# An FFN beside attention on one core: the weight operands of TensorE moved to different starting bytes

## The chip, the cores and the metric

The kernel runs on one core of a Trainium2 chip. The core has five engines that run side by side: TensorE (PE; its weight loads are listed apart as PEld), VectorE (DVE), ScalarE (ACT), GpSimd (POOL) and SyncE (SP), which here issues the transfers. Operands lie in an on-chip memory of 128 partitions; a tile takes the same bytes in each partition, so "address" below means a byte within a partition. The metric is device time in microseconds of one execution; smaller is better.

## The reference, cut to what matters

Two branches read the same x (2048 rows, 576 columns, fp32) and are mixed row by row with a sigmoid gate:

```
g = sigmoid((x * gate_w).sum(-1))
a = attention(x)            # 32 heads of 18, four segments of 512 rows, softmax inside a
                            # segment and a running memory across segments, then @ wo
b = (silu(x @ w_gate) * (x @ w_up)) @ w_down     # 576 -> 4608 -> 576
out = g * a + (1 - g) * b
```

The change touches the operands of branch b only: `w_gate`, `w_up` and `w_down`.

## The kernel before

All matrix products of the projections and of the FFN are done in split form. An fp32 operand becomes a high part (ScalarE copies it to the format `F32R`) and a low part (VectorE subtracts the high part from the original); three products, high by high, high by low and low by high, are added in PSUM.

The kernel has four stages. Up to about 229 us the projections q, k, v are computed (`qk`, `v_step`, both through `products`, line 138). From there the FFN runs in two halves of 1024 rows, up to about 935 and 1640 us, and the attention of all segments is dealt out between its matmuls. At the end the attention's output is multiplied by `wo` (again line 138) and mixed with the FFN's sums.

**The FFN's gate and up (line 1034).** `F` = 4608 is cut into 36 blocks of 128 columns (`f`). For one block the two halves of rows and the two matrices gate and up form a two by two problem, which is computed with seven products in place of eight: seven combinations of weights (`wops`, `j` = 0 to 6) against seven combinations of x (`XO[j]`). One product is six matmuls at line 1034 (two row tiles `z`, each with high·high, high·low, low·high) and a seventh at line 1037 for the last 64 rows of D (`rem`, tiles `rh0` and `rh1`). The weights are the **stationary** operand (128x128), x is **streamed** past them (512 columns).

The tile of one combination of weights is `wo_`, made by `op_tile` (line 216), 2048 bytes per partition: high and low part of two row tiles. The pool `wop` holds seven such places, taken in turn, and ahead of them `rh0` and `rh1`. In the first half the tiles are made by `w_make`: GpSimd forms sums (`total`, line 247), ScalarE writes the high part (line 251), VectorE the low part (line 254), and SP stores the tile to `wc` in DRAM (line 257). In the second half `w_fetch` (line 703) loads them from there. Four places also hold raw x for a while before the second half (`x_second`, line 1004).

**The FFN's down product (line 893).** `down_group` multiplies the activations `hh`, `hl` (stationary) by the split down weights `dw` (streamed, 320 or 256 columns): nine matmuls for three blocks `f`, three per block, into one PSUM bank, and VectorE adds the result to `ya` (line 898). `dw` holds high and low part side by side, 2 x 576 numbers or 4608 bytes; the pool `fp` has three places of it. `d_split` makes one in the first half, and SP stores it to `dc`; `d_fetch` loads it in the second.

**The order of the work** is written out by hand. `tick` and `beat` are called after each of the seven products; they run what `defer` put into a list for that beat (loads, splits, stores), then up to three groups of the down product and at times a step of the attention generator `att_gen`. So behind a product at 1034 and 1037 there follows another product, a group at 893, or bf16 matmuls of attention (lines 727, 748, 769, 798, 800).

**Addresses.** Pools are stacked from two ends. From the low end: the ring (1024 bytes), `consts`, `xo` (x and its combinations), `rw`, `fp` (`hh`, `hl`, `draw`, `dw`), `yp` (`ya`). From the high end: `base` (32 bytes), `rp` (raw weights), `wop`, and below it the attention's pools. Within a pool tiles lie in the order of their first request. Two small tiles, `gap` in `consts` and `base`, are there only to shift what follows. With these sizes `xo`, `hh`, `hl`, `dw`, `ya`, `rh` and `wo_` all begin on byte 192 modulo 256.

Of the kernel before, what the change touches and what calls it, by code (L numbers as in the profile page):

```python
# [12 lines left out]
F32 = mybir.dt.float32  # L13
F32R = mybir.dt.float32r
# [6 lines left out]
P = 128  # L21
S = 2048
D = 576
H = 32
DH = 18
L = 512
# [37 lines left out]
def gated_mix(ctx, tc, xT, xrest, wf, wfr, wfh, wd, wv, wo, beta, cmask, ident, bmask, out):  # L64
    nc = tc.nc
# [133 lines left out]
    def raw_tile():  # L199
        return rp.tile([P, L], F32, name="raw")  # L200
# [12 lines left out]
    wraw_of, wops, rhs = {}, {}, []  # L213

    def op_tile():
        return wop.tile([P, 2, 2, P], F32R, name="wo_")

    def r_block(h, o):
        i, c = divmod(h, 2)
# [19 lines left out]
    def w_make(f):  # L239
        g, u = wraw_of.pop(f)  # L240
        ops = wops[0, f] = [None] * 7
        a11, a12, a21, a22 = g[:, 0:2], g[:, 2:4], u[:, 0:2], u[:, 2:4]
        src = [a11, None, None, a12, None, None, a22]

        def total(j, p, q, sub=True):
            src[j] = rp.tile([P, 2, P], F32, name="ws", bufs=3)
            (nc.gpsimd.tensor_sub if sub else nc.gpsimd.tensor_add)(src[j], p(), q())  # L247

        def high(j):
            ops[j] = op_tile()  # L250
            nc.scalar.activation(ops[j][:, 0], src[j], AF.Copy)

        def low(j):
            nc.vector.tensor_sub(ops[j][:, 1], src[j], f32(ops[j][:, 0]))

        def keep(j):
            nc.sync.dma_start(wc[f, j], f32(ops[j]).rearrange("p a k n -> p (a k n)"))

        todo = [(LEAD - 1, lambda: total(1, lambda: a21, lambda: a22, False)),
                (LEAD, lambda: total(2, lambda: src[1], lambda: a11)),  # L260
                (LEAD + 2, lambda: total(4, lambda: a11, lambda: a21)),
                (LEAD + 4, lambda: total(5, lambda: a12, lambda: src[2]))]
        for j in range(7):
            todo += [(LEAD + j, lambda j=j: high(j)), (LEAD + j + 2, lambda j=j: low(j)),
                     (LEAD + j + 3, lambda j=j: keep(j))]
        return sorted(todo, key=lambda t: t[0])
# [3 lines left out]
    with ExitStack() as st:  # L270
# [192 lines left out]
        for kt in range(NT):  # L463
            if kt % 2 == 0:
                both = staging(), staging()
            a = both[0][:, L * (kt % 2):L * (kt % 2) + 3 * P].rearrange("p (m n) -> p m n", n=P)
# [118 lines left out]
        for s in range(NSEG):  # L585
            upd = upd_gen(s - 1) if s else None
            casts = []
            for n, (m, u) in enumerate(chains):
                mid = []
                if s == 0:  # L590
                    for z in loads.get(n, []):
                        z()
                    if 0 < n < 6:
                        mid.append(lambda n=n: q_split(*chains[n + 3]))
                    if n in halves:
                        mid.append(lambda n=n: v_split(*halves[n]))
                if s == 1 and n < 3:
                    cast = masks(*((0, 3), (3, NT), (0, 0))[n])
                    casts.append(cast)
                if s == 1 and 3 <= n < 6:  # L600
                    mid.append(casts[n - 3])
                if (s, n) == (1, 7):
                    mid.append(betas)
                if (s, n) == (0, 3):
                    b_load(0)
                if (s, n) > (0, 3) and blocks:
                    mid.append(lambda z=blocks.pop(0): b_step(*z))
                if 1 <= s < 3:
                    if n == 2:
                        rest_load(2 - s)  # L610
                    for j in RSTEP.get(n, ()):
                        mid.append(lambda j=j: rest_split(2 - s, j) if j >= 0 else rest_sum(-j))
                if s == 3:
                    if 2 <= n < 6:
                        first_load(n - 2)
                    for j, z in FSUM.get(n, []):
                        mid.append(lambda j=j, z=z: first_sum(j, z))
                    for j, z in FSPLIT.get(n, []):
                        mid.append(lambda j=j, z=z: first_split(j, z))
                if s < 3:  # L620
                    for kt in ((0, 1), (2, 3), (4,))[n - 6] if s == 0 and n > 5 else (n - 4,) if s and n > 3 else ():
                        raws["x", kt] = x_load(s + 1, kt)
                qk(s, m, u, mid)
                flush(2)
                if upd is not None and n > 0:
                    next(upd, None)
            if s == 3:
                qst_.close()
                rp = pool(ctx, "rp", 4, side="right")
                wop = pool(ctx, "wop", 7, side="right")  # L630
                kq = pool(ast, "kq", 1, side="right")
                for i in range(NST):
                    if i < 2:
                        qst.append(kq.tile([P, 2, L], BF, name=f"qst{i}"))
                    if i < NST - 1:
                        kst.append(kq.tile([P, 2, L], BF, name=f"kst{i}"))
                for i in range(2):
                    mbs.append(kq.tile([P, 8], F32, name=f"mb{i}"))
                for z in range(2):
                    for j, b, kt in ((0, 2, z), (3, 2, 2 + z), (5, 3, 2 + z)):  # L640
                        XO[j][z] = xs_of[b][0][kt]
                wraw_of[0] = [w_load(0, u) for u in range(2)]
                for z in range(2):
                    rhs.append(wop.tile([P, 7, P], F32R, name=f"rh{z}", bufs=1))
                start = w_make(0)
            for n in range(8):
                hf, i = divmod(n, 4)
                flush()
                v_step(s, hf, i)
                if s:  # L650
                    mem_step(s, n // 2, n % 2)
                if s < 3:
                    if n == 0:
                        xs_of[s + 1] = x_tiles(s + 1)
                    if 1 <= n < 6:
                        x_split(xs_of[s + 1], n - 1, raws["x", n - 1])
                else:
                    if n == 4:
                        wraw_of[1] = [w_load(1, u) for u in range(2)]
                    if n < 2:  # L660
                        first_sum(6, n)
                    elif n < 6:
                        if n < 4:
                            nc.gpsimd.memset(f32(rhs[n - 2][96:]), 0.0)
                        if 3 <= n < 5:
                            r_fetch(n - 3)
                        if n - 2 < len(kst):
                            nc.gpsimd.memset(kst[n - 2], -1.0)
                    if n > 2:
                        for z in stack_loads(0)[2 * n - 6:2 * n - 4]:  # L670
                            nc.sync.dma_start(*z)
                    for _ in range((0, 0, 2, 3, 3, 3, 3, 3)[n]):
                        if start[0][0] < 8:
                            start.pop(0)[1]()
# [7 lines left out]
    with ExitStack() as st:  # L682
# [9 lines left out]
        fp = pool(st, "fp", CH)  # L692
# [174 lines left out]
                nc.sync.dma_start(*z)  # L867

        def d_tile():
            return fp.tile([P, 2, D], F32R, name="dw")  # L870

        def d_split(f, r):
            d = d_tile()
# [124 lines left out]
        def x_second(new, rest):  # L998
            r = {}
            todo = []  # L1000

            def load(z, q):
                b, kt = ((0, z), (1, z), (0, 2 + z), (1, 2 + z))[q]
                r[z, q] = wop.tile([P, L], F32, name="wo_") if z else raw_tile()[:, :L]
                nc.sync.dma_start(r[z, q], xT[HALF[1][b], :, kt])

            def total(z, j):
                c, d, e, g = (r.get((z, q)) for q in range(4))
                o, p, q = {1: (c, d, c), 4: (d, g, d), 2: (g, g, c), 6: (e, e, g)}[j]
                nc.gpsimd.tensor_sub(o, p, q)  # L1010

            def parts(z, j):
                new[j][z] = x_slot(SLOT[j], z)
                split(new[j][z][:, 0], new[j][z][:, 1], r[z, (0, 0, 3, 2, 1, 3, 2)[j]])

            def fetch(j):
                rest[j] = xr_tile(j)
                nc.sync.dma_start(f32(rest[j]), xrd[j])

            todo += [(o, lambda z=z, q=q: load(z, q)) for o, z, q in LOADS]  # L1020
            todo += [(o, lambda z=z, j=j: parts(z, j)) for o, z, j in PARTS]
            todo += [(o, lambda z=z, j=j: total(z, j)) for o, z, j in SUMS]
            todo += [(6 + j, lambda j=j: fetch(j)) for j in range(7)]
            return sorted(todo, key=lambda t: t[0])
# [17 lines left out]
        for pos, (half, f) in enumerate(seq):  # L1042
            if f == 0:
                yas[half] = yp.tile([P, 8, D], F32, name="ya")
            q = f % CH
# [186 lines left out]
```

## Time and profile before

| | |
|---|---|
| median of 3 runs | 1804.82 us (1804.8 to 1804.99) |
| span of the profiled execution, first to last instruction | 1803.0 us |
| around the span (median less span) | 1.8 us |
| granted TensorE clock, mean | 0.997 |
| PE busy, 0 to 229 us / 229 to 935 / 935 to 1640 / 1640 to 1803 | 221.38 / 696.21 / 703.67 / 157.84 us |
| ACT busy, the same stretches | 147.15 / 400.62 / 362.00 / 50.21 us |
| POOL busy, the same stretches | 106.84 / 316.07 / 380.90 / 28.52 us |
| DMA share, the same stretches | 0.57 / 0.69 / 0.56 / 0.52 |

The profiled execution is one execution on the chip with every instruction's start and duration; its own time is known here only as its span, to which the 1.8 us around it are added for a comparison with the runs. Matmuls overlap, and their recorded ends are modelled, so a busy PE says little by itself: what counts is the distance from one matmul's start to the next one's. The chain of work that ended last, listed in order of time, gives just this, since each piece in it lasts until the next piece starts. In its rows stand the start, the length, the engine with the tile written, the line, and how many instructions were merged.

### The profile page before, as it was taken

The numbers are of one execution on the slowest core, as the hardware profiler recorded it, in microseconds if no ns is written. First come the engines' busy times: TensorE is split into PE (matmuls) and PEld (weight loads), VectorE is DVE, ScalarE is ACT, GpSimd is POOL, SyncE is SP. The second block draws the span as 40 slices with busy tenths as digits, with TensorE's granted clock in tenths as the row PEclk, the third lists the DMA queues.
The fourth block names the chain that finished last, engine by engine and source line by source line (L and its number), as shares of the span: only waits on it lengthen the run. The fifth ranks groups of instructions, "written<-read, shape, count | busy, mean of one in ns | idle before, by whom it ended". The sixth has DMA issues, their size and how long they took to land.

```text
span 1803.0 us, 36363 instructions
## 1 busy us (share of the span) xinstructions
PE 1779.1 (99%) x12444; PEld 1529.7 (85%) x12444; DVE 1269.7 (70%) x3257; ACT 960.0 (53%) x1799; POOL 832.3 (46%) x1065
## 2 busy tenths in 40 slices
PE   9999999999999999999989999999999999999999
PEld 7898978888888888888877888888887887888899
DVE  6566566778877777777777767777777777764455
ACT  7666564465556555655546465355355355354511
POOL 4434632345554455345535555555555555553121
PEclk9999999999999999999999999999999999999999
DMA  8643496777657756776478456466455455456644
GB/s 289 215 174 141 148 324 205 229 260 264 186 198 248 256 181 193 246 247 193 160 262 247 137 176 195 135 172 195 124 179 181 144 168 180 137 160 187 199 137 139
DMA packets 244073, 352.01 MB, mean 195 GB/s; under 512 B 83440, under 2 KB 125680, under 8 KB 243888
## 3 DMA queue, kind: packets, MB, share of 16 engines
q1 hardware_dynamic: 243888, 349.68, 60.3%
q8 instruction: 99, 1.62, 0.4%
q14 instruction: 86, 0.70, 0.1%
HBM read 210.72 MB, written 138.87 MB: 194 GB/s over the span
## 4 chain that ended last, share of the span: by engine, by line
PE 92%; DVE 2%; DMA 2%; ACT 2%; issue 1%; SPq 0%; POOL 0%; ACTq 0%; DVEq 0%
PE bank L1034 36%; PE bank L893 25%; PE bank L138 11%; PE bank L1037 6%; PE bank L769 4%; PE bank L727 4%; PE bank L798 2%; PE bank L800 1%; PE bank L446 1%; PE bank L400 1%; DMA wo__23682<-wc 0%; DVE xo L116 0%; DMA stk<-q 0%; PE bank L332 0%; DMA raw<-in_xT_dram 0%
## 5 line engine op out<-in xcount | busy, mean ns | idle before, releaser
L893 PE MATMUL bank<-dw,hh 128*128 128x320 f32 (+1 forms) x2304 | 486.5, 304 | 6.0 <-DVE ya L898 4.4
L863 POOL TENSOR_TENSOR p<-pe,p 128x512 f16<-128x512 f32 x320 | 382.7, 1196 | 155.5 <-DVE p L861 107.1
L893 PEld LDWEIGHTS bank<-dw,hh 128*128 128x128 f32 x2304 | 377.9, 189 | 24.8 <-DVE ya L898 6.3
L773 ACT ACTIVATE pe<-bank 128x512 f32<-128x512 f32 x320 | 190.3, 595 | 313.9 <-PE bank L769 285.5
L893 PE MATMUL bank<-dw,hl 128*128 128x320 f32 (+1 forms) x1152 | 340.2, 295 | 0.3 <-DVE hl L116 0.3
L781 POOL TENSOR_SCALAR_AFFINE_SELECT pe<-pe 128x256 f32<-128x256 f32 (+1 forms) x320 | 137.5, 430 | 293.7 <-ACT pe L773 289.8
L734 DVE CUSTOM_DVE_ANT_0 scr<-bank,cm 128x512 bf16<-128x512 f32 (+3 forms) x512 | 247.8, 484 | 20.0 <-PE bank L727 12.0
L898 DVE TENSOR_TENSOR ya<-bank,ya 128x320 f32<-128x320 f32 x352 | 157.9, 453 | 113.2 <-PE bank L893 110.8
L893 PEld LDWEIGHTS bank<-dw,hl 128*128 128x128 f32 x1152 | 217.6, 189 | 0.9 <-DVE hl L116 0.9
L1037 PE MATMUL bank<-xr,rh 128*128 128x512 f32 x504 | 196.8, 391 | 0.0
L861 DVE CAST p<-pe 128x512 f16<-128x512 f32 x320 | 152.3, 476 | 0.0
L769 PE MATMUL bank<-qst,kst 111*128 111x512 bf16 (+3 forms) x512 | 150.9, 303 | 0.0
L727 PE MATMUL bank<-kst,qst 108*128 108x512 bf16 (+3 forms) x512 | 126.0, 300 | 0.6 <-DVE mb L734 0.5
L247 POOL TENSOR_TENSOR ws<-raw 128x256 f32<-128x256 f32 x72 | 66.2, 920 | 108.0 <-DMA raw<-in_wf_dram 51.7
L977 DVE TENSOR_TENSOR hl<-row,hh 128x512 fp32r<-128x512 f32 x120 | 99.7, 831 | 18.9 <-ACT hh L976 18.4
L1037 PEld LDWEIGHTS bank<-xr,rh 128*128 128x128 f32 x504 | 94.7, 188 | 20.3
L1101 ACT ACTIVATE row<-bank 128x512 f32<-128x512 f32 x72 | 43.1, 599 | 122.3 <-PE bank L1037 122.3
L1106 DVE TENSOR_TENSOR row<-bank,row 128x512 f32<-128x512 f32 x72 | 49.8, 691 | 81.8 <-ACT bank L1105 81.8
L1116 DVE TENSOR_TENSOR row<-bank,row 128x512 f32<-128x512 f32 x72 | 49.7, 690 | 64.2 <-PE bank L1037 51.5
L1105 ACT ACTIVATE bank<-bank 128x512 f32<-128x512 f32 x72 | 41.9, 582 | 97.9 <-PE bank L1037 94.8
L138 PE MATMUL bank<-xo,qhi 128*128 128x512 f32 x264 | 83.1, 396 | 0.0
L1098 DVE TENSOR_TENSOR bank<-bank,row 128x512 f32<-128x512 f32 x72 | 50.2, 697 | 41.6 <-PE bank L1037 33.4
(1702 smaller groups left out, 4040.3 us busy)
## 6 DMA issues: line engine op xcount, KB each, us to landing
rh<-rc SPq DMA_DIRECT2D x72, 336.0 KB
dc<-dw SPq DMA_DIRECT2D x36, 576.0 KB
dw<-dc SPq DMA_DIRECT2D x36, 576.0 KB
raw<-in_wf_dram SPq DMA_DIRECT2D x72, 256.0 KB
stk<-q SPq DMA_DIRECT2D x32, 384.0 KB
draw<-in_wd_dram SPq DMA_DIRECT2D x36, 288.0 KB
rc<-rt SPq DMA_DIRECT2D x42, 224.0 KB
vd<-vps SPq DMA_DIRECT2D x8, 912.0 KB
```

The source lines that it names most:

```text
L138: nc.tensor.matmul(t, st[n], mv[n], start=(n == 0), stop=(n == 13))
L727: nc.tensor.matmul(t[:, c:c + w], qs[:KR, pr, P * i:P * i + P], ks[:KR, pr, 0:w], start=True, stop=True)
L734: nc.vector.tensor_tensor_reduce(scr[:, :w], t[:, c:c + w], cm[:, L - w:L], 1.0, -3.0e38, OP.add, OP.max, m[:, k:k + 1])
L769: nc.tensor.matmul(t[:, c:c + w], ks[:KR + 3, pr, P * j:P * j + P], qs[:KR + 3, pr, P * j:L], start=True, stop=True)
L773: nc.scalar.activation(pe, t, AF.Exp, scale=SCALE)
L781: nc.gpsimd.affine_select(d, d, pattern=pat, compare_op=OP.is_ge, fill=0.0, base=0, channel_multiplier=-1)
L861: nc.vector.tensor_copy(p1, pe)
L863: nc.gpsimd.tensor_sub(p2, pe, p1)
L893: nc.tensor.matmul(t, p, q[:, cs], start=(n == 0), stop=(n == 3 * CH - 1))
L898: nc.vector.tensor_add(ya[:, i, cs], t, ya[:, i, cs])
L1034: nc.tensor.matmul(t, w[:, p, z], x[z][:, q], start=first and n == 0, stop=False, skip_group_check=True)
L1037: nc.tensor.matmul(t, rem[:, RPOS[j]], XR[j], start=False, stop=True, skip_group_check=True)
```

## The change

It changes the size of two kinds of tiles, adds one small tile, and shrinks a reserved area. The tiles keep their shapes for all instructions: eight more numbers (32 bytes) are reserved behind each and cut off again in the same line. `wo_` grows from 2048 to 2080 bytes, so its seven places lie 2080 bytes apart; `dw` grows from 4608 to 4640 bytes. Eight numbers of `gap` stand between `rh1` and the first `wo_`. Together `wop` is 256 bytes longer (7 x 32 + 32), so that the pools below it move by a whole turn of 256. `dynamic_dma_scratch_size`, the ring at the low end of the memory, goes from 1024 to 256 bytes, which moves everything that is stacked from there by 768 bytes, three whole turns.

```diff
     def op_tile():
-        return wop.tile([P, 2, 2, P], F32R, name="wo_")
+        return wop.tile([P, L + 8], F32R, name="wo_")[:, :L].rearrange("p (a b c) -> p a b c", b=2, c=P)
...
                 for z in range(2):
                     rhs.append(wop.tile([P, 7, P], F32R, name=f"rh{z}", bufs=1))
+                wop.tile([P, 8], F32, name="gap", bufs=1)
                 start = w_make(0)
...
         def d_tile():
-            return fp.tile([P, 2, D], F32R, name="dw")
+            return fp.tile([P, 2 * D + 8], F32R, name="dw")[:, :2 * D].rearrange("p (a b) -> p a b", b=D)
...
-                r[z, q] = wop.tile([P, L], F32, name="wo_") if z else raw_tile()[:, :L]
+                r[z, q] = wop.tile([P, L + 8], F32, name="wo_")[:, :L] if z else raw_tile()[:, :L]
                 nc.sync.dma_start(r[z, q], xT[HALF[1][b], :, kt])
...
-    nc = _bacc.Bacc("TRN2", target_bir_lowering=False, num_devices=1, dynamic_dma_scratch_size=1024)
+    nc = _bacc.Bacc("TRN2", target_bir_lowering=False, num_devices=1, dynamic_dma_scratch_size=256)
```

## The prediction

> **What bounds the kernel now.** The page first: busy time by engine, then the chain of work that ended last.
>
> ```profile
> span 1803.0 us, 36363 instructions
> PE 1779.1 (99%) x12444; PEld 1529.7 (85%) x12444; DVE 1269.7 (70%) x3257; ACT 960.0 (53%) x1799; POOL 832.3 (46%) x1065
> PE 92%; DVE 2%; DMA 2%; ACT 2%; issue 1%; SPq 0%; POOL 0%; ACTq 0%; DVEq 0%
> PE bank L1034 36%; PE bank L893 25%; PE bank L138 11%; PE bank L1037 6%; PE bank L769 4%; PE bank L727 4%; PE bank L798 2%; PE bank L800 1%; PE bank L446 1%; PE bank L400 1%; DMA wo__23682<-wc 0%; DVE xo L116 0%; DMA stk<-q 0%; PE bank L332 0%; DMA raw<-in_xT_dram 0%
> ```
>
> TensorE sets the end: 92% of the chain is its own matmuls, one behind another. Two lines, 61% of the chain, read exactly the operands that the change moves: L1034 (weights of gate and up, stationary) and L893 (split down weights, streamed). So a count of nanoseconds per matmul decides, not a count of instructions. The clock is no variable, nearly all of it is granted:
>
> ```profile
> core 0: 1803.0 us, clock 0.997
> ```
>
> The step of one matmul is read from the chain in order of time (start, length, line, how many). Two stretches, undisturbed and disturbed:
>
> ```profile
> 418.40 0.23 PE bank L769
> 418.63 0.22 PE bank L727 x2
> 418.85 1.40 PE bank L1034 x6
> 420.25 0.23 PE bank L1037
> 420.48 1.37 PE bank L1034 x6
> 421.85 0.23 PE bank L1037
> 422.08 1.36 PE bank L1034 x6
> 423.44 0.23 PE bank L1037
> 423.66 1.36 PE bank L1034 x6
> ```
>
> Six matmuls of 512 columns take 1.40 us right behind the bf16 matmuls of attention, 1.37 in the next product, and then 1.36 for as long as nothing comes between. It settles into a step of 1.36/6 = 226.7 ns. The view of L1034 by tile (duration ns min/median/max) says the same:
>
> ```profile
> L1034 PE MATMUL bank<-xo,wo__2612 x6: 389/389/389, 240.5 to 241.7; 128*128 128x512 f32 x6
> L1034 PE MATMUL bank<-xo,wo__3671 x6: 389/394/397, 331.0 to 332.2; 128*128 128x512 f32 x6
> ```
>
> In the settled stretch all six last 389 ns to the nanosecond; beside attention they scatter from 389 to 397 with no engine awaited. I read this as a rhythm between the streamed operand and the next weight load, into which TensorE falls when each matmul meets the same arrangement as the last. Adding up the tile sizes gives that arrangement: in before x (`xo`), the remainders (`xr`, `rh`), all seven `wo_` places, `hh`, `hl` and all three `dw` places begin on byte 192 modulo 256. In the pieces of 15 us into which I cut 225 to 1710 us, 447 of the 504 sixes stand whole. 202 take 1.36 us (first and last below), 236 take 1.37 to 1.41, most 1.38 or 1.39; the other nine hold a cut edge or a stall.
>
> ```profile
> 240.69 1.36 PE bank L1034 x6
> ...
> 1705.19 1.36 PE bank L1034 x6
> ```
>
> ```profile
> 237.46 1.39 PE bank L1034 x6
> ...
> 1700.40 1.39 PE bank L1034 x6
> ```
>
> **The change, part by part.** No instruction, wait or DMA is added, removed or moved to another place in a queue: SP's and POOL's order stays. Only addresses change. The stated bytes come from the sizes: `rh` stays on 192, 32 bytes of gap follow, and the places, 2080 bytes apart, begin on 224, 0, 32, 64, 96, 128 and 160; `dw`, 4640 bytes apart, on 192, 224 and 0; `ya` behind it moves from 192 to 32. The rest moves by 768 or 256 bytes, whole turns.
>
> *Gate and up, 3,024 matmuls.* Six matmuls now have weights on one byte, the seventh (`rh`) on 192, the next six on another. If the rhythm hangs on that byte, it is broken twice in each product, and the settled six fall to what a disturbed six takes: 1.39 against 1.36. Settled are 202 of 447, on 504 some 228; 228 x 0.03 = **+6.8 us**. Above, the dearest kind among disturbed ones bounds it:
>
> ```profile
> 1099.99 1.41 PE bank L1034 x6
> ...
> 1102.14 1.41 PE bank L1034 x6
> ```
>
> All settled sixes at 1.41 are 228 x 0.05 = 11.4, and the 236 others (on 504: 266) from 1.385 to 1.41 another 6.7: +18 us. Below, nothing excludes a gain; its bound is in the rivals.
>
> *Split down weights, 3,456 matmuls.* Within nine matmuls the streamed byte changes after three and after six.
>
> ```profile
> 343.12 1.07 PE bank L893 x9
> ...
> 414.42 1.05 PE bank L893 x9
> ```
>
> ```profile
> 329.89 0.23 PE bank L727 x2
> 330.13 1.08 PE bank L893 x9
> ...
> 337.04 1.31 PE bank L893 x9
> ```
>
> Nines of 256 columns run 1.05 to 1.08 (84 whole ones: 45 at 1.07; the other 39 average 1.063), nines of 320 run 1.31 or 1.32. Here the settled value is not the cheapest, so an upset costs nothing: 192 nines x -0.007, some -1 us, between -3.8 (all from 1.07 to 1.05) and +1.9 (to 1.08). I take **-1**.
>
> *`ya`, the ring, and the transfers.* Taken at nothing, with this cover:
>
> ```profile
> PEld bank L893 <- DVE ya L898: 6.3, 8, 1.4
> PE bank L893 <- DVE ya L898: 4.4, 6, 1.2
> L898 DVE TENSOR_TENSOR ya<-bank,ya 128x320 f32<-128x320 f32 x352 | 157.9, 453 | 113.2 <-PE bank L893 110.8
> q1 hardware_dynamic: 243888, 349.68, 60.3%
>   DMA wo__23682<-wc: 0.4, 1
> ```
>
> DVE sums into `ya` 352 times at 453 ns and waits 110.8 us for TensorE there, while TensorE waits 10.7 us for it in all; if `ya` on byte 32 were 5% slower (23 ns), those 14 waits would grow by 0.3 us. The ring I take at nothing because every transfer that the kernel issues is in q1, the hardware's queue with 243,888 packets; the page's only other queues fetch instructions. The fetches of `wo_` and `dw` now land on multiples of 32 bytes. The second half fetches each product's weights a whole step ahead, and L1034 waited for such a landing once, 0.4 us. If a landing took several us longer that cover would go, and the 252 fetches would show as waits of L1034.
>
> **Sum.** +6.8 - 1.0 = +5.8 us on the span, 1808.8. The median of the runs stands 1.8 us above the span (1804.82 against 1803.0), so **1810.6 us**, taken as 1810.
>
> **The rivals.** *The byte doesn't matter: 1805 us, 0.27.* For it speak matmuls whose streamed operand already starts on other bytes. `wo0` and `wo1` (L138 at the end) have slices 1152 bytes apart, so they begin on 192 and 64 by turns, under weights on 192:
>
> ```profile
> 1783.58 3.73 PE bank L138 x28
> 1783.03 0.44 PE bank L952 x4
> 1787.85 3.72 PE bank L138 x28
> ```
>
> 28 matmuls of 288 columns in 3.72 us are 132.9 ns each. The straight line through 1.07/9 = 118.9 ns at 256 and 1.31/9 = 145.6 at 320 gives 132.2 there: two different bytes cost 0.7 ns, as good as nothing. Against it: 64 and 192 are only one pair of the eight, the weights themselves stood on 192 in every one of these rows, and 512 columns, the form with the settled step, never ran on differing bytes. The Trainium skill ("TensorE: Matmul & The Clock Gate", Step-by-step: what each phase is for) says that TensorE reads the streamed operand and the weights through two independent ports, so that loading the next weights takes nothing from the running matmul; by that rule this rival holds. The trace agrees only in part, since 389 to 397 ns and 1.36 to 1.41 us show something that meets. In this case I also count that the places do not come out on seven bytes (an allocator that rounds to 64 would give four), since even multiples of 64 then repeat what L138 shows.
>
> *Equal bytes are what costs: faster, 0.28.* The same line puts a fixed 118.9 - 256 x 0.417 = 12 ns on every matmul beside its columns (0.417 = (145.6 - 118.9)/64; at 512 it gives 225.7, measured 226.7). If that is the weight load and the stream, both on 192, reaching the same part of the memory at once, then the new places, none of them on 192, take part of it away at L1034. Each ns is 3,024 x 1 = 3.0 us, so it decides from 1.2 ns (3.6 us) on. A quarter of the 12 ns, 3 ns, gives -9 us, **1796**; half would give 1787. For it: all matmuls of L1034 and L893 run on equal bytes and all pay those 12 ns. Against it: L138, where bytes differ in half the matmuls, pays the 12 ns in full.
>
> *Slower, the forecast: 0.45.* For it: the settled step is the shortest six that the rows show, is seen only behind products of the same kind, and takes one product or two to find again after a break; seven places on seven bytes make every product unlike its neighbour. Against it: whether the rhythm depends on the weights' byte at all is not shown, as they never stood on another.
>
> **How the numbers follow.** A measurement of this kernel can tell about 0.2%, 3.6 us, from no change. Chances: slower by more 0.45, within it 0.27, faster by more 0.28. The forecast's own range is 1808.5 to 1822 (+18 on 1804.8). With the other cases the range runs from 1794 (a quarter and a little more of the 12 ns) to 1820: it leaves out about 0.1 below (half or more of the 12 ns) and 0.05 to 0.1 above (every six at its dearest, with late landings).
>
> **What would show it.** Right: the sixes of 1.36 us in the chain become rare, most at 1.38 to 1.41; median durations of L1034 by tile move from 389 to 392 to 397 ns, also in the long undisturbed stretches such as 430 to 441 us; L138 and the nines of L893 keep their lengths within 0.02 us. The second rival right: 1.36 stays as frequent as now. The third right: undisturbed sixes under 1.35 us, on other tiles than `rh`'s. Wrong in its cover: new waits of L1034 for `wo_` from `wc`, of L893 for `ya`, or `ya` sums far from 453 ns. The whole argument would be wrong if the time moved while the sixes and nines kept their lengths.

## The result, and the profile after

| | before | after |
|---|---|---|
| median | 1804.81 us (1804.07 to 1804.99, 4 runs) | 1812.69 us (1811.96 to 1814.15, 4 runs) |
| ratio to before, 95% interval | | 1.0045 (1.003 to 1.006) |
| span of the profiled execution | 1803.0 us | 1810.2 us |

The changed kernel is slower by 0.45%, 7.9 us. First its page: the span, busy time by engine, the chain of work that ended last by engine and by line, and the sums into `ya`. One line has been added at 645, so every later line is one higher than before: 1034 is now 1035, 1037 is 1038, 893 is 894.

```profile
span 1810.2 us, 36363 instructions
PE 1788.6 (99%) x12444; PEld 1528.1 (84%) x12444; DVE 1273.0 (70%) x3257; ACT 961.3 (53%) x1799; POOL 833.0 (46%) x1065
...
PE 94%; DVE 3%; ACT 1%; DMA 1%; issue 1%; SPq 0%; POOL 0%; DVEq 0%; ACTq 0%
PE bank L1035 38%; PE bank L894 24%; PE bank L138 10%; PE bank L1038 6%; PE bank L770 4%; PE bank L728 4%; PE bank L799 2%; PE bank L801 1%; PE bank L446 1%; PE bank L400 1%; DVE xo L116 0%; DMA xo<-in_xT_dram 0%; PE bank L332 0%; DMA stk<-q 0%; PE bank L953 0%
...
L899 DVE TENSOR_TENSOR ya<-bank,ya 128x320 f32<-128x320 f32 x352 | 157.9, 453 | 111.3 <-PE bank L894 108.9
```

The granted clock, from the view of the cores:

```profile
core 0: 1810.2 us, clock 0.997
```

The instructions are the same in number and the clock is the same. PE's busy time grew by 9.5 us, the share of gate and up in the chain from 36 to 38%. DVE, ACT and POOL stand within a few us of where they were, the sum into `ya` on its new byte takes the same 453 ns, and no wait for a weight tile from DRAM stands among the chain's lines that the page lists (`DMA wo__23682<-wc` was there before). So the time lies in TensorE's own matmuls; the table below says in which.

The chain in order of time, in a stretch where nothing comes between the products of gate and up:

```profile
432.12 1.40 PE bank L1035 x6
433.52 0.23 PE bank L1038
433.75 1.37 PE bank L1035 x6
435.12 0.23 PE bank L1038
435.36 1.40 PE bank L1035 x6
```

Before, such a stretch fell to 1.36 after two products and stayed there. Here it does not settle: 1.40, with one product in seven at 1.37. Counted as in the prediction, in pieces of 15 us from 225 to 1710 us, before had 202 sixes at 1.36, 16 at 1.37, 79 at 1.38, 117 at 1.39 and 24 at 1.40 or 1.41. After has none at 1.36, 23 at 1.37, 24 at 1.38, 112 at 1.39, 263 at 1.40 and 30 at 1.41. The view of L1035 by tile (duration ns min/median/max) for the same stretch, behind one row of a much earlier product:

```profile
L1035 PE MATMUL bank<-xo,wo__2613 x6: 392/395/404, 239.8 to 240.9; 128*128 128x512 f32 x6
...
L1035 PE MATMUL bank<-xo,wo__5086 x6: 392/394/397, 430.3 to 431.5; 128*128 128x512 f32 x6
L1035 PE MATMUL bank<-xo,wo__5100 x6: 393/395/397, 432.0 to 433.1; 128*128 128x512 f32 x6
L1035 PE MATMUL bank<-xo,wo__5114 x6: 388/392/394, 433.6 to 434.7; 128*128 128x512 f32 x6
L1035 PE MATMUL bank<-xo,wo__5120 x6: 390/394/399, 435.2 to 436.4; 128*128 128x512 f32 x6
L1035 PE MATMUL bank<-xo,wo__5136 x6: 392/395/404, 436.8 to 438.0; 128*128 128x512 f32 x6
L1035 PE MATMUL bank<-xo,wo__5157 x6: 391/394/400, 438.5 to 439.6; 128*128 128x512 f32 x6
L1035 PE MATMUL bank<-xo,wo__5173 x6: 392/396/398, 440.1 to 441.2; 128*128 128x512 f32 x6
```

No median is 389 any more. The seven rows carry seven different triples, and in this half of the FFN an undisturbed product mostly shows that of its place: `wo__2613`, 200 us earlier in the same place as `wo__5136`, shows 392/395/404 too. The seven places do differ, as the change says.

To book the whole difference I add up, over all 12,444 matmuls, the time from one start to the next, by the line of the first of the two:

| line before (columns) | before, us | after, us | difference |
|---|---|---|---|
| 1034 (512) | 715.57 | 725.86 | +10.3 |
| 1037 (512) | 122.39 | 121.45 | -0.9 |
| 893 (256) | 221.09 | 219.83 | -1.3 |
| 893 (320) | 266.30 | 266.35 | 0.0 |
| 138 (288) | 99.41 | 97.66 | -1.8 |
| all others | 373.3 | 374.1 | +0.8 |
| sum | 1798.0 | 1805.2 | +7.2 |

The -1.8 of line 138 lies in a wait and the steps behind it 40 to 46 us into the span, before any operand of the change is read. The six other variants of the kernel profiled below have 96.7 to 98.1 us there, so before's execution is the odd one. The rest is L1034's loss, less a little from the nines of 256 columns.

### The profile page after: what moved, and what is told of

Its sections match the earlier page's. It is cut to its first block, busy times and chain, and to the rows that moved or that the text cites. A ratio compares the mean times of both kernels' runs of the same rounds, so it can differ in the third digit from the quotient of the medians.

```text
span 1810.2 us, 36363 instructions
## 1 busy us (share of the span) xinstructions
PE 1788.6 (99%) x12444; PEld 1528.1 (84%) x12444; DVE 1273.0 (70%) x3257; ACT 961.3 (53%) x1799; POOL 833.0 (46%) x1065
## 4 chain that ended last, share of the span: by engine, by line
PE 94%; DVE 3%; ACT 1%; DMA 1%; issue 1%; SPq 0%; POOL 0%; DVEq 0%; ACTq 0%
PE bank L1035 38%; PE bank L894 24%; PE bank L138 10%; PE bank L1038 6%; PE bank L770 4%; PE bank L728 4%; PE bank L799 2%; PE bank L801 1%; PE bank L446 1%; PE bank L400 1%; DVE xo L116 0%; DMA xo<-in_xT_dram 0%; PE bank L332 0%; DMA stk<-q 0%; PE bank L953 0%
## 5 line engine op out<-in xcount | busy, mean ns | idle before, releaser
L1106 ACT ACTIVATE bank<-bank 128x512 f32<-128x512 f32 x72 | 41.9, 582 | 98.1 <-PE bank L1038 95.0
L138 PE MATMUL bank<-xo,qhi 128*128 128x512 f32 x264 | 83.1, 396 | 0.0
```

What stands on the lines that cost most here:

```text
L138: nc.tensor.matmul(t, st[n], mv[n], start=(n == 0), stop=(n == 13))
```

## The experiments

Two theories could explain that loss. **Unlike neighbours** is the forecast's: TensorE's short step is a rhythm that breaks when the weights' byte changes from product to product. **Distance** is its rival: the step depends on how far the weights' starting byte lies from the streamed operand's, modulo 256, in each matmul by itself, and 0 is a cheap distance. In before every operand of these lines stood on 192, at distance 0. After the change the seven places stand at distances 32, 64, 96, 128, 160, 192 and 224 from x: none is at 0. A third thing to settle was which of the two parts, `wo_` or `dw`, makes the difference.

### TensorE alone, at stated distances

`m1_bytes` has only matmuls: 36 or more in a row with the same kind of operands as L1034 and L893, in one piece per distance, and four small bf16 matmuls between pieces. The piece's start for the weights is moved by the distance d.

```
    for n in (512, 320, 256):
        for d in range(0, 256, 32):
            run(n, [(d, 0)] * 36)          # (byte of weights, byte of x)
    ...
    for d in (32, 64, 128):
        run(512, ([(d, 0)] * 6 + [(0, 0)]) * 6)
    run(512, [(d if i < 6 else 0, 0) for d in (32, 64, 96, 128, 160, 192, 224) for i in range(7)])
    run(512, [(d, 0) for d in (32, 64, 96, 128, 160, 192, 224) for i in range(7)])
    run(512, [(d, d) for d in range(0, 224, 32) for i in range(7)])
```

> A kernel of TensorE alone: it leaves the whole computation out and writes zeros. x and w begin on the same byte modulo 256; runs of 36 fp32r matmuls with 128x128 weights follow one another, each parted from the next by four bf16 matmuls. The weights begin 0, 32, 64, ... 224 bytes behind x's byte, for 512, 320 and 256 columns; then at 4, 8, 16 and 48 bytes, then with x moved instead, then in the pattern of a product (six moved, the seventh not), then the byte changing from seven to seven as in the changed kernel. Theory 1 (unlike neighbours: what counts is that each matmul meets the same arrangement as the last): every run at one constant distance settles at 226.7 ns, 36 in 8.16 us, whatever the distance; only the runs that change within themselves take 231 to 235 ns a matmul. Theory 2 (distance: the settled step depends on how far the weights' byte is from x's): 8.16 us at 0, other lengths, 8.3 to 8.5 us, at most other distances. Theory 3 (the byte plays no part in TensorE, the cause is traffic of other engines): all runs of 512 columns 8.16 us.

Its chain, pieces only (the rows between are the small matmuls). The first three are 512 columns at distances 32, 96 and 192; then 320 columns at 0 and 32; then 256 columns at 0 and 224.

```profile
24.12 8.45 PE bank L93 x36
...
41.51 8.47 PE bank L93 x36
...
67.60 8.31 PE bank L93 x36
...
84.84 5.33 PE bank L93 x36
...
90.40 5.34 PE bank L93 x36
...
129.42 4.36 PE bank L93 x36
...
161.37 4.26 PE bank L93 x36
```

The first piece, at distance 0, begins with steps of 572, 426 and 427 ns, as no other piece does, and can't be read as a whole; the same piece is shown under `m2_fine`. For the table I take the mean step of the last twelve matmuls of each piece, from their starts:

| distance | 0 | 32 | 64 | 96 | 128 | 160 | 192 | 224 |
|---|---|---|---|---|---|---|---|---|
| 512 columns, ns | 226.67 | 233.33 | 233.33 | 234.6 | 233.33 | 233.33 | 228.83 | 233.33 |
| 320 columns, ns | 146.67 at all eight | | | | | | | |
| 256 columns, ns | 120.0 | 118.3 | 117.75 | 118.5 | 118.25 | 120.0 | 117.75 | 116.67 |

With 512 columns a constant foreign byte settles too, on a mean that is mostly 6.67 ns higher (single steps by turns 231 to 235 ns at distance 32, 226 or 227 at 0). Moving x by 32 in place of the weights gives 233.3 as well, by 64 (the same distance as the weights on 192) 228.8, and by 128 232.5 where the weights gave 233.33: the distance decides, to 1 ns, and not which operand is moved. In the product pattern, six moved and one not, distances alone would give (6 x 233.33 + 226.67)/7 = 232.4 ns, and 232.0 with the seven distances of the changed kernel; measured without the first six steps were 232.8, 233.3 and 232.4 at 32, 64 and 128, and 232.8 in the changed kernel's own pattern. So a change of byte from product to product adds at most 1 ns where the distances are foreign anyway, and most distances add 6.67 ns to every settled matmul. One thing stayed unclear: where both operands moved together every seven matmuls, the groups on 64, 128 and 192 settled at 226.7 and those on 32, 96 and 160 did not within seven (229.6 over all). It is taken up below.

### One part of the change at a time

`e1_gate_up_only` is the change without its edit of `dw`:

```diff
-            return fp.tile([P, 2 * D + 8], F32R, name="dw")[:, :2 * D].rearrange("p (a b) -> p a b", b=D)
+            return fp.tile([P, 2, D], F32R, name="dw")
```

> The changed kernel with the three places of dw as before (4608 bytes apart, all on 192). All theories of TensorE's step: the 3,024 matmuls of gate and up carry the loss, so 1812 to 1815 us, about 1 us above the changed kernel since the nines of 256 columns give their 1.3 us back. If it is the down weights or ya that cost: 1804 to 1806 us.

`e2_down_only` is the reverse: `dw` and the ring as in the change, and `wo_` back on 192. These are before's lines, with the change's one edit:

```diff
-            return fp.tile([P, 2, D], F32R, name="dw")
+            return fp.tile([P, 2 * D + 8], F32R, name="dw")[:, :2 * D].rearrange("p (a b) -> p a b", b=D)
```

> The kernel before with the three places of dw on 192, 224 and 0, ya on 32, and the ring of 256 bytes; wo_ stays on 192. Theories 1 and 2 of the step at gate and up: 1803 to 1805 us, a gain of up to 1.5 us from the nines of 256 columns. If the down weights, ya or the ring cost: 1808 to 1813 us.

Both ran on another chip than the change, beside before (1803.3 us, 15 runs): `e1_gate_up_only` 1813.52 us (1812.22 to 1814.81), ratio 1.0055 (1.0042 to 1.0068); `e2_down_only` 1800.83 us (1798.7 to 1802.13, 11 runs), ratio 0.9983 (0.9974 to 0.9992). The whole loss is gate and up's. The part with `dw` alone is a small gain, 2.5 us where up to 1.5 was expected. In the chain of the first, the undisturbed stretch:

```profile
434.09 1.40 PE bank L1035 x6
...
435.72 1.40 PE bank L1035 x6
```

In the chain of the second, the last product of such a stretch, and behind it two nines:

```profile
325.04 1.36 PE bank L1034 x6
...
326.63 1.31 PE bank L893 x9
...
328.17 1.08 PE bank L893 x9
```

L1034 takes 725.47 us in `e1_gate_up_only` and 715.14 in `e2_down_only`. The nines of 256 columns are 221.32 and 219.76: they follow `dw`. `e1_gate_up_only` is not measurably slower than the change itself (the intervals overlap), so what `dw` gives in the change is of the size of its -1.3 us. In `e2_down_only` the ring has 256 bytes and `ya` lies on 32, and it is faster than before: neither costs anything that shows. Its smaller ring also moves x by 768 bytes against the weights `wo_`, which stay; that is three turns of 256, and L1034 stays within 0.5 us of before, so whole turns change nothing.

### The same foreign byte for all

The theories part here. `e3_all_on_224` puts all seven `wo_` places and both `rh` on byte 224. No product is unlike its neighbour, and every matmul of L1034 and L1037 is at distance 32. `dw` stays on 192.

```diff
+                pad = pool(ctx, "pad", 1, side="right")
+                nc.gpsimd.memset(pad.tile([P, 56], F32, name="pad"), 0.0)
...
+                wop.tile([P, 8], F32, name="gap", bufs=1)
```

> The kernel before with all seven places of wo_ and both of rh on byte 224, x and everything else on 192, the ring of 256 bytes: one constant distance of 32 bytes. Theory 1 (unlike neighbours): the rhythm comes back, about 200 whole sixes of 1.36 us, 1804 to 1806 us. Theory 2 (distance): no six settles at 1.36 us, most stay at 1.38 to 1.41, 1810 to 1818 us.

It took 1815.98 us (1815.26 to 1816.8), ratio 1.0069 (1.0056 to 1.0081), L1034 727.49 us. Its chain (L1037 is before's L1034):

```profile
432.06 1.40 PE bank L1037 x6
...
433.69 1.40 PE bank L1037 x6
...
435.33 1.40 PE bank L1037 x6
```

Here all are at 1.40, and counted over the whole FFN as above 94 are at 1.39, 347 at 1.40 and none is shorter. By the starts, the 234 sixes that took at most 1.365 us before now take 233.3 or 233.4 ns in each of their six steps on the mean, as with TensorE alone. "Unlike neighbours" falls as the cause of the loss: with nothing changing from product to product the whole loss is there. L1034 loses 1.6 us more than in the change (the intervals of the two ratios overlap, so the times alone don't tell them apart). That fits the table: every product pays 6.67 ns, while in the change the place at distance 192 pays only 2.2 (there are 432 matmuls on it, 432 x 4.5 ns = 1.9 us).

### A cheap distance other than 0?

`m2_fine` repeats the measurement at all 32 distances in steps of 8 bytes, for 512, 288 and 256 columns, behind 120 small matmuls where `m1_bytes` had 40. The step of these small ones falls from 107 to 56 ns after the first 26; in `m1_bytes` they took 107 up to the last, and the first piece began with the long steps.

```
    between(120)
    for n in (512, 288, 256):
        for d in range(0, 256, 8):
            run(n, [(d, 0)] * 36)
```

> TensorE alone again, the computation left out and zeros written: runs of 36 matmuls with the weights 0, 8, 16, ... 248 bytes behind x's byte, for 512, 288 and 256 columns. Distance theory: at 512 columns 0 stays at or near the shortest (8.16 us for 36), most others at 8.4 us, 192 near 8.24; at 256 columns 0 is one of the longest (4.32 us), 224 the shortest of the multiples of 32 (4.20 us). Nothing is forecast for 288 columns but that the step lies between 130 and 137 ns. If only whole blocks of 32 bytes count, the four distances inside a block agree; in the first such kernel 8 bytes gave 230.6 and 16 gave 233.3 ns, so I expect that they don't.

Its chain, 512 columns at distances 0, 64 and 192:

```profile
18.79 8.24 PE bank L93 x36
...
87.70 8.45 PE bank L93 x36
...
226.29 8.32 PE bank L93 x36
```

With 512 columns, again over the last twelve, 226.67 ns at 0, 16, 120 and 240; 228.8 at 192; 233.3 at 16 others and 230.0 to 234.3 at the last eleven. But distance 16 had 233.33 in `m1_bytes`, so its short step here was not to be relied on; those at 120 and 240 were measured only this once. With 288 columns 130.0 to 136.7 (131.7 at 0), with 256 from 113.3 (88 and 168) to 120.4.

`e5_gate_up_on_128` tests the one multiple of 32 that had come out between, distance 192: `wo_` and `rh` all on 128.

```diff
+                pad = pool(ctx, "pad", 1, side="right")
+                nc.gpsimd.memset(pad.tile([P, 16], F32, name="pad"), 0.0)
...
+                wop.tile([P, 48], F32, name="gap", bufs=1)
```

> The kernel before with all places of wo_ and rh on byte 128, x on 192: one constant distance of 192. Distance theory: TensorE alone took 228.8 ns there against 226.7 at 0 and 233.3 at 32, so a little slower than before and clearly faster than with 224: 3,528 matmuls by 0 to 2.1 ns, ratio 1.000 to 1.004, sixes mostly 1.37 to 1.38 us. If any distance other than 0 is alike: ratio 1.006 to 1.008, as with 224.

1806.42 us (1804.61 to 1807.45, 11 runs), ratio 1.0019 (1.001 to 1.0028), L1034 719.71 us: 4.1 us over before, where (228.83 - 226.67) x 3,024 would be 6.5 if before had always been settled. Its chain:

```profile
432.87 1.37 PE bank L1037 x6
...
434.47 1.37 PE bank L1037 x6
```

The kernel's time follows the distance, with equal neighbours in all three cases: 0 (before), 192 (1.0019), 32 (1.0069).

### Equal bytes elsewhere

In before every operand of these lines stood on a multiple of 64. Is it the distance, or the byte 192 itself? `m4_together` moves both operands alike, then puts distance 32 at other places, then alternates groups of 14, then enters distances 16 and 0 behind 4 to 11 small matmuls.

```
    for d in range(0, 256, 32):
        run(512, [(d, d)] * 36)
    for d in (8, 16, 24, 48):
        run(512, [(d, d)] * 36)
    for d in range(32, 256, 32):
        run(512, [(d, d - 32)] * 36)
    ...
    for d in (32, 64):
        run(512, ([(d, 0)] * 14 + [(0, 0)] * 14) * 2)
    for c in range(4, 12):
        between(c - 4)
        run(512, [(16, 0)] * 36)
    ...
```

> Only matmuls on TensorE, the computation is left out and zeros are written. 512 columns, both operands moved alike by 0 to 224 bytes, 36 matmuls in a row; then distance 32 at seven different places; then alternating groups of 14; then distance 16 and distance 0, eight times each, entered after different numbers of small matmuls. If only the distance counts, every piece with equal bytes settles at 226.7 ns per matmul, wherever it lies, and every piece at distance 32 at 233.3. If the place itself counts (bytes on odd multiples of 32 cost something even at distance 0), the pieces moved alike by 32, 96, 160 and 224 stay above 229. Groups of 14 at alternating distances 32 and 0 should run at 233.3 and 226.7 but for a few transition steps. If distance 16 has two settled steps chosen by the entry, some of its eight pieces show 226.7 and some 233.3, while all eight at distance 0 show 226.7.

Rows of its chain: both operands moved by 0, by 32, by 8, and then the first piece at distance 32:

```profile
19.59 8.26 PE bank L93 x36
...
28.08 8.23 PE bank L93 x36
...
87.42 8.43 PE bank L93 x36
...
122.19 8.46 PE bank L93 x36
```

All eight pieces on equal multiples of 32 settle at 226.67. All seven at distance 32 settle at 233.33, wherever they lie. So the groups of seven in `m1_bytes` were only too short to settle. Groups of 14 at distances 32 and 0 by turns run, in their last eight steps, at 233.4, 226.6, 233.4 and 226.6. In groups of 14 with both operands moved alike, by turns on 0 and 32 or on 0 and 64, the distance is always 0; yet each change of bytes is followed by 3 to 10 steps of up to 236 ns before 226.67 comes back, and the groups take 227.5 to 230.0 on the mean. So a change of byte does upset the short step for a while; what the step settles to is set by the distance. Two more things came out otherwise than a bare distance would have it: both moved by 8, 16, 24 or 48 settle at 232.8, 233.3, 236.7 and 231.1, so equal bytes are cheap only on multiples of 32; and distance 16 has 233.33 behind every entry tried, so they do not explain its 226.67 in `m2_fine`.

`e6_both_on_224` is the kernel before with everything moved by 32 bytes from both ends of the memory: `xo`, `hh`, `hl`, `dw`, `ya`, `rh` and `wo_` all begin on 224.

```diff
-    nc.gpsimd.memset(base.tile([P, 8], F32, name="base"), 0.0)
+    nc.gpsimd.memset(base.tile([P, 64], F32, name="base"), 0.0)
...
-    consts.tile([P, 16], F32, name="gap")
+    consts.tile([P, 24], F32, name="gap")
```

> The kernel before with everything in the on-chip memory moved by 32 bytes modulo 256, from both ends: x, the weights of gate and up, hh, hl, dw and ya all begin on 224, at distance 0. If the distance alone counts, the time is that of before: ratio 0.999 to 1.001, with some 234 sixes at 1.36 us. If the byte itself counts (224 is an odd multiple of 32, and every operand of before stands on a multiple of 64), the sixes of 1.36 are gone and the ratio is 1.003 to 1.007, as with the weights alone on 224.

1804.17 us (1801.07 to 1807.36, 11 runs) beside 1804.07, ratio 1.0 (0.9991 to 1.001). Its chain has the short sixes again, 186 at 1.36 where before had 202; L1034 takes 716.98 us, 1.4 more than before and 10.5 less than with the weights alone on 224:

```profile
304.52 1.36 PE bank L1034 x6
...
306.11 1.36 PE bank L1034 x6
```

With the weights alone on 224 the kernel took 1.0069; with x on 224 as well it takes 1.000. The distance decides, not the byte.

### The down weights

`e4_down_on_224` puts all three `dw` places on byte 224. There `dw` is the stream, and the weights `hh`, `hl` on 192 are at distance 224 from it, the cheapest for 256 columns in `m1_bytes`.

```diff
+            if not gaps:
+                gaps.append(fp.tile([P, 8], F32, name="gap", bufs=1))
+            d = fp.tile([P, 2, D], F32R, name="dw")
+            if len(gaps) == 1:
+                gaps.append(fp.tile([P, 56], F32, name="pad", bufs=1))
+            return d
```

> The kernel before with all three places of dw on byte 224, hh and hl (the weights of that product) on 192, everything else on before's byte, the ring of 256 bytes: a distance of 224 from stream to weights. Distance theory, from the first measurement of TensorE alone (256 columns: 120.0 ns at 0, 116.7 at 224; 320 columns: 146.7 at both): 1,728 matmuls by 1.6 to 3.3 ns shorter, 2.7 to 5.7 us, so a ratio of 0.9968 to 0.9985; nines of 256 columns at 1.05 us. Theory of unlike neighbours: no change, ratio 0.999 to 1.001.

1801.09 us (1799.3 to 1803.2, 11 runs), ratio 0.9989 (0.998 to 0.9998) against 1803.31 us. Chain rows of two pairs of nines (L900 is before's L893):

```profile
326.44 1.32 PE bank L900 x9
327.99 1.07 PE bank L900 x9
...
330.66 1.32 PE bank L900 x9
332.21 1.06 PE bank L900 x9
```

The 256-column nines fall to 219.04 us (-2.1), those of 320 rise by 0.5. That is a smaller gain than the expected ratio of 0.9968 to 0.9985, which the interval just reaches, and it does not beat `e2_down_only`; the two intervals overlap. `m3_nines` asks TensorE alone whether nines, which are short, have a better distance than 224. Ahead of them it has pieces of 36 with 320 columns, which take 145.0 ns at distance 120, 148.8 at 168 and 146.5 to 147.1 at all others.

```
    for d in range(0, 256, 8):
        for n in (320, 256, 320, 256):
            run(n, [(d, 0)] * 9)
```

> TensorE alone, the computation left out and zeros written: for each distance 0, 8, ... 248 first 36 matmuls of 320 columns, then nines of 320, 256, 320, 256 columns with four bf16 matmuls between, as the down product has them. Distance theory: the nines of 256 columns are shortest at 88 and 168 bytes, where long runs took 113.3 ns against 120.0 at 0: some 0.03 to 0.06 us less for a nine. Nines are short, so that part of the difference may not show; long runs of 320 columns took 146.7 at all multiples of 32 and should vary by 2 ns at most. A distance is worth trying in the kernel where both nines together are at least 0.03 us under those at 0 (192 pairs: 5.8 us).

A pair of nines at distance 0 and a pair at 224, from its chain:

```profile
200.32 1.38 PE bank L93 x9
...
201.94 1.13 PE bank L93 x9
...
363.85 1.37 PE bank L93 x9
...
365.46 1.11 PE bank L93 x9
```

By the starts a pair takes 2.540 us at 224, the shortest of the 32, and 2.558 to 2.567 at 0. Of the two short steps for 256 columns, that of distance 88 is not seen in nines (1.165 us against 1.160 at 0), that of 168 is (1.117), but there the nine of 320 is the longest of all (1.429 against 1.407 at 0), so the pair takes 2.546. 192 pairs at 0.02 us would be 4 us; the nines of the kernel got 1.5. With one byte for both widths no version beyond `e2_down_only` and `e4_down_on_224`, 0.1 to 0.2% under before, was pointed to. A byte of their own for the 256 columns alone was not tried.

## Why the prediction was right, and which step of it was not

**Direction and size** held: 1810.6 worked out, 1812.69 measured, slower by 7.9 us where +5.8 was forecast.

**The settled sixes.** The term was 228 sixes losing 0.03 us, +6.8. By the starts 234 sixes took at most 1.365 us before; the same 234 are 0.034 us longer after, +7.9 us. The term stood.

**The other 270 sixes** were taken at nothing and lost 0.009 us each, +2.4. This is the part of the sum that was too small. It has the same cause: a six behind attention or a nine settles while it runs. Its last two steps took 229.5 and 229.2 ns on the mean before, 233.4 and 231.7 after, and 234.0 and 233.4 in `e3_all_on_224`. The bound of +18 left room for it.

**The reason given for the settled sixes failed.** The step read "if the rhythm hangs on that byte, it is broken twice in each product, and the settled six fall to what a disturbed six takes". The loss is not the breaking: `e3_all_on_224` changes no byte from product to product and loses at least as much as the change, and in `m1_bytes` a constant foreign byte settles at 233.33. A change of byte does upset the short step, as the groups at distance 0 in `m4_together` show, but the changed kernel had no short step left to upset. What the change took away was the distance 0 between weights and stream, and each product pays for its own distance. That the number came out was luck: a disturbed six in before, 1.39, happens to lie beside six steps of 233.3 ns, 1.40. I had read the 389 ns rows as "settled" against "disturbed". They carried the distance too, but no row of before with 512 columns had another one to show it. A count of the new places' distances, none of them 0, would have given all 504 sixes rather than 228.

**Equal bytes are what costs** had the sign reversed where most of the matmuls are: at 512 columns the equal bytes are the cheapest distance of the eight. At 256 columns it was right, 120.0 ns at distance 0 and 116.67 at 224, and that is where the change's small gain lies. Of the 12 ns beside the columns that this rival wanted to take away, no distance took any at 512 columns; at 256 a distance in steps of 32 took at most 3.3.

**The byte doesn't matter** is refuted for 512 columns and holds for 320 in steps of 32, 146.67 at all eight distances. Its evidence was L138's 28 matmuls of 288 columns at one other distance. That form spreads from 130.0 to 136.7 ns over the distances in `m2_fine`, so one pair of bytes could not speak for the others, nor one width for another. The Trainium skill ("TensorE: Matmul & The Clock Gate", Step-by-step: what each phase is for) says that stream and weights come through two independent ports, so that loading the next weights takes nothing from the running matmul. These runs show that the two do depend on each other, to 3% of a step: the same matmuls, with TensorE alone at work, take 226.7 or 233.3 ns by the distance between the two operands. Whether they meet at the ports or elsewhere is not shown.

**The split down weights**: -1 forecast, -1.3 measured. They have a better and a worse distance; that they came out a little better was not the upset of a settled value but the 116.7 to 118 ns of the foreign distances against 120.

**`ya`, the ring and the transfers** cost nothing, as forecast: 453 ns per sum, and the waits of TensorE for it stand as they did, in the waits of after:

```profile
PEld bank L894 <- DVE ya L899: 6.5, 8, 1.4
PE bank L894 <- DVE ya L899: 4.6, 6, 1.2
```

That is 11.1 us against 10.7, and no wait of L1035 for `wo_` from `wc` stands in that view. The output's product at the end kept its length too:

```profile
1786.52 3.72 PE bank L138 x28
```

**Open.** Why distance 0 is cheap at 512 columns, on multiples of 32 alone, and dear at 256 was not found. 226.67, 233.33, 146.67 and 120.0 are 34, 35, 22 and 18 times 6.667 ns, which looks like a grid on which a matmul's start must fall; that is a remark on numbers, and no run tested it. Of the 2.5 and 2.2 us that `e2_down_only` and `e4_down_on_224` gain, 1.3 and 2.1 are booked in the nines of 256 columns. The wait early in the run and L1037 also differ there, and were not separated.

## What to carry to other kernels

Where a kernel is bound by a row of like matmuls, the starting bytes of the two operands are a parameter like any other, here worth 3% of a step and up to 0.7% of the kernel: measure the step for the kernel's own width over the distances, with TensorE alone and in pieces as long as the kernel's, before choosing addresses. A settled step in a profile tells of one arrangement only, and rows that all share one distance can't say whether it is the cheap one. When a change moves several things at once (here each place's byte and the likeness of neighbours), count first in how many instructions each of them differs from before.

## What the runs showed of the hardware

- An F32R matmul of 512 columns with 128x128 weights takes 226.67 ns per step, TensorE alone and settled, if weights and stream begin on the same byte modulo 256 and that byte is a multiple of 32; 228.8 at distance 192, and 233.33 at five of the six other multiples of 32 (234.6 at 96). Which multiple of 32 the common byte is changes nothing.
- After both operands have moved to another common byte, the short step of 512 columns came back only after 3 to 10 matmuls (`m4_together`).
- The same does not hold for other widths: 146.67 ns for 320 columns at all multiples of 32, 116.67 to 120.0 for 256, with equal bytes among the dearest.
- At distance 16 one piece of 512 columns settled at 226.67 ns and nine others at 233.33. What chooses is open.
